# A third place for score products and products of zeros in TensorE's first waits, in a planned attention and mixture kernel

One Trainium2 chip, one core. The metric is the device time of one execution in microseconds (us), median of several runs; less is better.

## The reference

```python
# q, k, v: (8, 12, 448, 64)
scores = scale * np.matmul(q, k.transpose(0, 1, 3, 2))
m = np.max(scores, axis=-1, keepdims=True)
e = np.exp(scores - m)
attn = e / (np.sum(e, axis=-1, keepdims=True) + np.exp(-m) + 1e-09)
x = (attn @ v), heads side by side                # (3584, 768)
h = x @ w_in                                      # 768 -> 2048
P = a[0] + a[1] * h + a[2] * h**2 + a[3] * h**3
Q = 1.0 + np.abs(b[0]) * np.abs(h) + np.abs(b[1]) * h**2
out = (P / (Q + 1e-06)) @ w_out                   # 2048 -> 768
```

## The kernel before

The kernel writes its instructions in an order that a small planner in its own source finds while the kernel is built: every piece of work is an `Op` with an engine, an assumed duration and what it depends on, and `Plan.run` simulates the engines and takes the op that can start first. Twelve heads of a batch are three *quads* of four heads. For each quad TensorE makes eight score passes (K times Q, two heads side by side in two row tiles), ScalarE (ACT) takes exponentials of them, TensorE makes the sums (ones, then V in two halves), VectorE (DVE) multiplies by the reciprocal, and later come the dense products of x and w_in and of g and w_out. Score passes before batch 1 are cut in halves of 224 columns, so batch 0 has six half quads.

PSUM has eight banks: two score places of two banks each, `sps`, and four general banks, `gen`, for transposes, sums and dense products.

```python
sps = [ps.tile([128, 2, 512], F32, name=f"sps{i}") for i in range(NS)]      # NS = 2
gen = [ps.tile([128, 512], F32, name=f"gen{i}") for i in range(NGEN)]       # NGEN = 4
# ... in scores(), simplified:
    nc.tensor.matmul(
        out=sps[m % NS][0:128, hh, ci * qw:(ci + 1) * qw],
        lhsT=kt[n % NK][r, c0:c0 + 128],
        rhs=qt[n % NK][r, pr * S + q0:pr * S + q0 + qw], start=True, stop=True)
    nc.scalar.activation(out=e_sb[m % NE], in_=sps[m % NS][0:P, :, 0:S],
                         func=AF.Exp, scale=scale)
# ... from batch 3 on, passes are held back until two can go together:
    if b >= MB and t % 2:
        ops[t - 1].mate = s
```

The planner's knobs are tables of numbers: when each quad's attention is due (`DUE`, `DUES`), how far the products with w_out lag (`LAG`), and in which order weights and K, Q, V are loaded (`ORDER`; i is a piece of w_in, o of w_out, k is K and Q of a quad, v is V).

The softmax here doesn't subtract the row's maximum and nothing guards it: scores larger than these inputs give would overflow.

## Time and profile before

| | before |
|---|---|
| time, median of 4 runs | 431.44 us (430.86 to 431.57) |
| span of the profiled run | 429.0 us |
| TensorE / DVE / ACT busy | 418.3 / 339.7 / 327.9 us |
| products (matmul instructions) | 3680 |
| changes of kind on TensorE | 235 |
| time at full pace for all products | 386.8 us |

The last row is worked out: each product is given its columns at 2.4 GHz and 2.5 ns, as the Trainium skill has it ("TensorE: Matmul & The Clock Gate", "Wait — 56ns, not 53.3ns?"), halved for scores and transposes and quartered for sums, which run two and four side by side. That is 189 ns for 448 columns, where the trace shows 0.190. TensorE's records name their kind by source line, so a *change of kind* is a pair of neighbouring records of different kind among transposes, scores, sums and dense products (the first record is counted as one; where a kernel makes products of zeros, these count as a fifth kind).

From these two I read every trace as a ledger: the useful work that TensorE has done by a given moment, and the changes that it has paid for. What is left of a stretch after its useful work and 0.105 us per change was lost to waits or to a slow clock.

### The profile page before, as it was taken

The page shows a single profiled execution, that of the slowest core. Times are in us where ns is not written, and L with a number is a line of the kernel's source. Part 1 is how long each engine was busy: PE and PEld are TensorE (multiplying, and loading weights), DVE is VectorE, ACT ScalarE, POOL GpSimd, SP SyncE. Part 2 cuts the span into 40 slices and gives each one's busy share as a digit, 9 for nine tenths or more (in the row PEclk, how much of TensorE's full clock was granted, in tenths as well). Part 3 has the DMA queues.
Part 4 walks back from the last instruction along what each step waited for, and adds up shares of the span by engine and source line. Part 5 has one row for each costly group of instructions (what it writes and reads, how often), then busy time and mean ns, then how long its engine had stood idle before and what let it go on. Part 6 is the DMA issues. An engine that isn't in the chain of part 4 may idle for free.

```text
span 429.0 us, 8850 instructions
## 1 busy us (share of the span) xinstructions
PE 418.3 (98%) x3680; PEld 218.5 (51%) x3680; DVE 339.7 (79%) x513; ACT 327.9 (76%) x383; POOL 109.3 (25%) x170
## 2 busy tenths in 40 slices
PE   5899999999999999999999999999999999999996
PEld 2666664444444444455444455444444455555663
DVE  4437999999989997559987489984999999979500
ACT  4898999988999999744999984878878865585421
POOL 6555534543535203421206102320000100100000
PEclk9999999999999999999999999999999999999999
DMA  9999999999949833976339628914010101211222
GB/s 198 203 202 199 192 174 178 187 169 167 131 89 102 103 69 58 118 135 129 72 41 136 84 49 132 138 37 81 2 37 2 38 0 38 73 34 41 75 73 76
DMA packets 78185, 43.58 MB, mean 102 GB/s; under 512 B 36160, under 2 KB 74560, under 8 KB 78144
## 3 DMA queue, kind: packets, MB, share of 16 engines
q0 software_dynamic: 36928, 21.89, 38.9%
q1 hardware_dynamic: 39952, 20.26, 25.3%
q10 hardware_dynamic: 1264, 0.85, 0.7%
q8 instruction: 29, 0.48, 0.4%
q14 instruction: 12, 0.10, 0.1%
HBM read 45.62 MB, written 11.01 MB: 132 GB/s over the span
## 4 chain that ended last, share of the span: by engine, by line
PE 81%; DVE 14%; ACT 2%; DMA 1%; issue 1%; ACTq 0%; DVEq 0%
PE gen L716 33%; PE gen L618 29%; PE gen L552 11%; PE sps L517 8%; DVE h L635 3%; DVE n L655 2%; DVE n L659 2%; ACT e L525 2%; DVE c L659 1%; DMA g<-in_k_dram 1%; DVE g L659 1%; DVE x L580 1%; DVE c L655 1%; DVE w L655 1%; PE gen L433 0%
## 5 line engine op out<-in xcount | busy, mean ns | idle before, releaser
L525 ACT ACTIVATE e<-sps 112x896 f16<-112x896 f32 x192 | 167.5, 922 | 25.0 <-PE sps L517 24.2
L618 PE MATMUL gen<-x,w_in 128*128 128x448 f16 (+1 forms) x864 | 161.5, 332 | 0.0
L716 PE MATMUL gen<-w_out,g 128*128 128x384 f16 (+2 forms) x768 | 134.9, 326 | 0.0
L618 PEld LDWEIGHTS <-w_in 128*128 128x128 f16 x864 | 79.6, 98 | 70.8 <-issue 17.4
L716 PEld LDWEIGHTS <-g 128*128 128x128 f16 x768 | 73.3, 98 | 56.4 <-issue 7.5
L635 DVE CAST h<-gen 128x448 f16<-128x448 f32 x113 | 68.9, 617 | 19.0 <-PE gen L618 18.7
L659 DVE TENSOR_TENSOR n<-n,h 128x1792 f16<-128x1792 f16 x64 | 69.9, 1092 | 0.9
L670 ACT ACTIVATE c<-c,oneeps_c 128x1792 f16<-128x1792 f16 x32 | 57.4, 1794 | 16.2 <-DVE c L659 16.2
L738 ACT ACTIVATE o<-gen 128x384 f32<-128x384 f32 (+2 forms) x56 | 27.5, 492 | 44.6 <-PE gen L716 44.6
L517 PE MATMUL sps<-qt,kt 64*128 64x448 f16 (+1 forms) x432 | 57.9, 341 | 2.5 <-ACT e L525 1.2
L673 ACT ACTIVATE c<-c 128x1792 f16<-128x1792 f16 x32 | 54.7, 1709 | 0.3
L693 POOL COPY gx<-g 128x1024 f16<-128x1024 f16 x8 | 9.4, 1172 | 154.7 <-DVE g L659 154.7
L580 DVE TENSOR_TENSOR x<-gen,lden 128x448 f16<-128x448 f32 (+1 forms) x54 | 28.3, 563 | 21.1 <-ACT lden L568 17.1
L655 DVE TENSOR_SCALAR n<-n,abc 128x1792 f16<-128x1792 f16 x64 | 44.1, 689 | 1.0
L552 PE MATMUL gen<-e,vn 112*32 112x448 f16 (+1 forms) x864 | 41.8, 337 | 0.0
L659 DVE TENSOR_TENSOR g<-n,c 128x1792 f16<-128x1792 f16 x32 | 35.1, 1095 | 7.1 <-ACT c L673 6.2
L659 DVE TENSOR_TENSOR c<-c,w 128x1792 f16<-128x1792 f16 x32 | 35.0, 1094 | 0.1
L517 PEld LDWEIGHTS <-kt 64*128 64x128 f16 x432 | 14.7, 95 | 36.5 <-issue 33.1
L318 POOL DMA_DIRECT2D vn<-in_v_dram x24 | 18.1, 755 | 57.4 <-PE sps L517 43.9
L478 POOL COPY kp<-kn 112x256 uint32<-112x256 uint32 x36 | 19.5, 573 | 44.5 <-DMA kt<-kp 41.4
L552 PEld LDWEIGHTS <-vn 112*32 112x32 f16 x864 | 23.1, 99 | 14.0
L655 DVE TENSOR_SCALAR n<-h,abc 128x1792 f16<-128x1792 f16 x32 | 25.5, 797 | 0.3
(45 smaller groups left out, 249.2 us busy)
## 6 DMA issues: line engine op xcount, KB each, us to landing
vn<-in_v_dram POOLq DMA_DIRECT2D x24, 224.0 KB, 7.3
kn<-in_k_dram POOLq DMA_DIRECT2D x22, 224.0 KB, 7.8
qn<-in_q_dram POOLq DMA_DIRECT2D x22, 224.0 KB, 8.3
w_in<-in_moe_w_in_dram POOLq DMA_DIRECT2D x12, 256.0 KB, 10.2
w_out<-in_moe_w_out_dram POOLq DMA_DIRECT2D x4, 768.0 KB, 16.9
out_dram<-o SPq DMA_DIRECT2D x8, 336.0 KB, 3.2
out_dram<-o SPq DMA_DIRECT2D x8, 288.0 KB, 2.7
out_dram<-o SPq DMA_DIRECT2D x7, 240.0 KB, 2.5
```

The source lines that it names most:

```text
L517: nc.tensor.matmul(out=sps[m % NS][0:(P if i == 0 and j == 1 else 128), hh, ci * qw:(ci + 1) * qw], lhsT=kt[n % NK][r, c0:c0 + (P if i == ...
L525: nc.scalar.activation(out=e_sb[m % NE], in_=sps[m % NS][0:P, :, 0:S], func=AF.Exp, scale=scale)
L552: nc.tensor.matmul(out=gen[unit["bank"]][32 * h:32 * h + 32, 0:qw], lhsT=lhs(h, j), rhs=e_sb[m % NE][:, h % 2, c0:c0 + qw], start=(j == 0) ...
L580: mult.emit = lambda s=s, uu=uu: nc.vector.tensor_tensor(out=x_sb[b % NX][:, 2 * qd + s, q0:q0 + qw], in0=gen[uu["bank"]][:, 0:qw], in1=ld ...
L618: nc.tensor.matmul(out=gen[unit["bank"]][:, fi * qw:(fi + 1) * qw], lhsT=w_in_sb[wg][:, c // 2, c % 2, (fc % FG) * 128:(fc % FG + 1) * 128 ...
L635: nc.vector.tensor_copy(out=dst, in_=src)
L655: return lambda: nc.vector.tensor_scalar(out=out, in0=in0, scalar1=s1, scalar2=s2, op0=op0, **kw)
L659: return lambda: nc.vector.tensor_tensor(out=out, in0=in0, in1=in1, op=ALU.mult)
L670: lambda: nc.scalar.activation(out=c, in_=c, func=AF.Ln, bias=oneeps_c)))
L673: lambda: nc.scalar.activation(out=c, in_=c, func=AF.Exp, scale=-1.0)))
L716: nc.tensor.matmul(out=gen[unit["bank"]][:, 0:wd], lhsT=lhs, rhs=w_out_sb[f][:, fc % FG, cols], start=(fc == 0), stop=(fc == NFC - 1))
L738: nc.scalar.activation(out=o[:, cols], in_=gen[unit["bank"]][:, 0:wd], func=AF.Copy)
```

## The change

Three things are intended. A score pass that finds no free place may write two free general banks instead, one per head; then its exponential is cut in two, and the passes of a quad can be issued as 2, 3 and 3 instead of four times 2, from batch 2 on. While TensorE waits in the first 15.5 us, it makes products of a tile of zeros, so that its clock is released earlier. And all tables are found anew, with a planner that now counts TensorE at half pace up to 15.5 us.

```diff
+WAIT = 0.2 ... COLD = 15.5 ... WARM = 6.5 ... FILL = 0.048      # cut
+    def places(self, op):
+        out = [(h.end + 0.2 if h else 0.0, (i,)) for i, h in enumerate(self.slots)
+               if h is None or h.start is not None]
+        banks = self.bank_times()
+        if op.slot[2] and len(banks) >= GP:
+            out.append((banks[GP - 1][0] + 0.01, (banks[0][1], banks[1][1])))
+        return sorted(out)
...
+    def emit_fill(op, gap):
+        cols = op.dest()
+        for _ in range(int((gap - 0.08) / (FILL * (2 if op.start < WARM else 1)))):
+            nc.tensor.matmul(out=cols[0:64, 0:P], lhsT=idle[0:P, 0:64], rhs=idle[0:P, :],
+                             start=True, stop=True)
...
-    DUES = (0, 0, 4.2, 3.0)
+    DUES = (0, 0, 3.8, 3.8, 3.8, 0, 0, 0)
+    GROUPS = (2, 1, 3, 1, 1, 3, 1, 1)
+    START = ("ta tb s1 tc s0 s2 td s3 s5 s4 te A0 s7 s6 tf tg s9 s8 "
+             "A1 s10 s11 tl s12 s13 A2 s14 s15 s16 s17 A3 s18 s19 s20 s21 A4 s23 s22")
-    ORDER = "kikiikivkkvoovoovkvv"
+    ORDER = "kivkkvikiikovooovkvv"
...                                                # DUE and LAG: all values new
+                for hh in range(2):
+                    nc.scalar.activation(out=e_sb[m % NE][:, hh],
+                                         in_=gen[un["place"][hh]][0:P, 0:S],
+                                         func=AF.Exp, scale=scale)
...
     for op in plan.order:
+        if op.eng == "PE" and op.start < COLD:
+            if op.dest and op.start > end + 0.2:
+                emit_fill(op, op.start - end)
+            end = op.end if op.start < WARM else op.end - op.dur
         op.emit()
```

In `START`, s is a score pass, t a group of transposes, A the sums of a half quad. `op.dest` is the buffer that the op after the zeros will write.

More of the change, by code (lines that the diff above doesn't have):

```diff
@@ L24, in __init__ @@
         self.opens, self.kb, self.mode, self.lat = opens, kb, mode, lat
-        self.mate = None
+        self.slot = self.dest = None
+        self.group = 1
         self.start = self.end = self.land = None
@@ L31 @@
 SWITCH = 0.095
-WAIT = 0.5
+WAIT = 0.2
+GP = 2
+E_TWO = 0.2
+COLD = 15.5
+WARM = 6.5
+FILL = 0.048
 KB_US = 0.0027
@@ L49, in __init__ @@
         self.banks = [None] * banks
+        self.slots = [None, None]
         self.mode = None
@@ L99, in candidates @@
                 t = max(t, s[0])
+            if op.slot is not None:
+                places = self.places(op)
+                if not places:
+                    continue
+                s = places[0]
+                t = max(t, s[0])
             t = max(t, self.free[e])
@@ L104, in candidates @@
                 late = op.due > t
-                if name == "att" and op.mate is not None:
-                    tm = self.ready(op.mate)
-                    late |= tm is None or tm > t + WAIT
+                if op.group > 1:
+                    late |= len(places) < op.group or places[op.group - 1][0] > t + WAIT
                 if op.opens:
@@ L157, in run @@
             op.start = t
-            op.end = t + op.dur
+            op.end = t + op.dur * (2 if e == "PE" and t < COLD else 1)
             if e == "PE" and op.mode != self.mode:
@@ L165, in run @@
             self.pos[e, name] += 1
-            if s is not None:
+            if op.slot is not None:
+                unit, holder, _ = op.slot
+                unit["place"] = s[1]
+                if len(s[1]) == 1:
+                    self.slots[s[1][0]] = holder
+                else:
+                    holder.dur += E_TWO
+                    for i in s[1]:
+                        self.banks[i] = holder
+            elif s is not None:
                 _, unit, holder = op.gen
@@ L214 @@
     ones = const.tile([128, 32], F16, name="ones")
+    idle = const.tile([128, P], F16, name="idle")
     abc = const.tile([128, 6], F32, name="abc")
@@ L248, with place @@
     gen = [ps.tile([128, 512], F32, name=f"gen{i}") for i in range(NGEN)]
+    def place(unit, hh):
+        pl = unit["place"]
+        return gen[pl[hh]] if len(pl) > 1 else sps[pl[0]][:, hh]
     plan = Plan({
@@ L265, in emit_ident @@
         make_identity(nc, ident)
+    def emit_fill(op, gap):
[3 more added lines that the diff above has]
+                             start=True, stop=True)
     def emit_consts():
+        nc.vector.memset(idle, 0.0)
         nc.vector.memset(ones, 1.0)
@@ L289 @@
     PER = 1.95
-    DUES = (0, 0, 4.2, 3.0)
-    LEAD = 50.9
-    MB = 3
+    DUES = (0, 0, 3.8, 3.8, 3.8, 0, 0, 0)
+    GROUPS = (2, 1, 3, 1, 1, 3, 1, 1)
+    GB = 1
+    LEAD = 72.5
+    MB = 2
+    START = ("ta tb s1 tc s0 s2 td s3 s5 s4 te A0 s7 s6 tf tg s9 s8 "
+             "A1 s10 s11 tl s12 s13 A2 s14 s15 s16 s17 A3 s18 s19 s20 s21 A4 s23 s22")
     DUE = (
-        28.1, 39.7, 51.4, 58.5, 76.4, 91.4, 103.2, 87.5, 118.5,
-        129.9, 148.0, 129.5, 202.0, 155.9, 169.8, 134.0, 237.8, 280.8,
-        283.4, 262.8, 327.3,
+        29.7, 32.6, 39.6, 9.9, 62.9, 39.7, 101.8, 123.5, 140.9,
+        140.4, 169.9, 160.4, 189.3, 148.7, 221.8, 246.2, 253.0, 273.1,
+        291.1, 274.3, 297.0,
     )
     NPE = 6
-    TLEAD = 4.6
+    TLEAD = 0.1
     ACM = 100
@@ L445, in transpose_by_pe @@
                     src_op = first_casts[n, ti, pr, jh] if n < 2 else ld[n]
-                    tr = Op(f"t{n}", "PE", 0.4 / nh,
+                    tr = Op(f"t{n}", "PE", 0.21 / nh,
                             [src_op, ident_op, hist(qk_free, n, NK)], emit,
                             gen=(True, un, cp), mode="t")
+                    tr.dest = lambda un=un: gen[un["bank"]]
                     trs.append(tr)
@@ L510, in scores, with emit @@
                 chunks = [cc * jc + c for c in range(cc)]
-                def emit(pr=pr, chunks=chunks, m=m):
+                un = {}
+                def emit(pr=pr, chunks=chunks, un=un):
                     for ci, j in enumerate(chunks):
@@ L517, in emit @@
                             nc.tensor.matmul(
-                                out=sps[m % NS][0:(P if i == 0 and j == 1 else 128), hh,
-                                                ci * qw:(ci + 1) * qw],
+                                out=place(un, hh)[0:(P if i == 0 and j == 1 else 128),
+                                                  ci * qw:(ci + 1) * qw],
                                 lhsT=kt[n % NK][r, c0:c0 + (P if i == 0 and j == 1 else 128)],
@@ L522, in emit, with emit_e @@
                                 start=True, stop=True)
-                def emit_e(m=m):
-                    nc.scalar.activation(out=e_sb[m % NE], in_=sps[m % NS][0:P, :, 0:S],
-                                         func=AF.Exp, scale=scale)
+                def emit_e(m=m, un=un):
+                    if len(un["place"]) == 1:
+                        nc.scalar.activation(out=e_sb[m % NE],
+                                             in_=sps[un["place"][0]][0:P, :, 0:S],
+                                             func=AF.Exp, scale=scale)
+                        return
+                    for hh in range(2):
+                        nc.scalar.activation(out=e_sb[m % NE][:, hh],
+                                             in_=gen[un["place"][hh]][0:P, 0:S],
+                                             func=AF.Exp, scale=scale)
                 t = len(ops)
-                due = quad_due(n) + DUES[t // 2] * PER if b else 0.0
-                s = Op(f"s{m}", "PE", 0.19, ready_for(n, pr, jc, q0) + [hist(e_ops, m, NS)], emit,
+                due = quad_due(n) + DUES[t] * PER if b else 0.0
+                s = Op(f"s{m}", "PE", 0.19, ready_for(n, pr, jc, q0), emit,
                        due=due, mode="s", opens=t == 0 and i > 0)
                 ops.append(s)
-                if b >= MB and t % 2:
-                    ops[t - 1].mate = s
-                e_ops.append(plan.add("e", Op(f"e{m}", "ACT", 0.8,
-                                              [s, table, hist(e_free, m, NE)], emit_e,
-                                              due=due)))
+                if b >= MB:
+                    s.group = GROUPS[t]
+                e = plan.add("e", Op(f"e{m}", "ACT", 0.8, [s, table, hist(e_free, m, NE)],
+                                     emit_e, due=due))
+                s.dest = lambda un=un: place(un, 0)
+                s.slot = un, e, (t > 1 or i == 0) and b >= GB
+                e_ops.append(e)
         if q0 + qw == S:
@@ L564, in attend @@
                gen=(True, ud, ln), mode="a")
+        d.dest = lambda: gen[ud["bank"]]
         ln.deps = [d, hist(mults, i, 2)]
@@ L814 @@
     first = [op for op in trs[0] if not op.late]
-    late = [op for op in trs.pop(0) if op.late]
+    steps = {"ta": first[:2], "tb": first[2:3], "tc": first[3:], "td": trs[1][:2],
+             "te": trs[1][2:], "tf": trs[2][:2], "tg": trs[2][2:],
+             "tl": [op for op in trs[0] if op.late]}
+    halves_ = 2 * NQ
     prev = None
-    for i in range(len(units)):
+    for i, (b, qd, _, _) in enumerate(units):
         m0 = len(e_ops)
         passes = scores(i)
-        nu = units[i + 1] if i + 1 < len(units) else None
-        nxt = trs.pop(NQ * nu[0] + nu[1], []) if nu else []
-        if nu and nu[0]:
-            for op in nxt:
-                op.due = quad_due(NQ * nu[0] + nu[1]) - TLEAD
-                plan.add("tr", op)
-            nxt = []
-        more = {}
-        if i == 0:
-            more = {-1: first[:2], 0: first[2:3], 1: first[3:], 2: nxt[:2]}
-            rest = nxt[2:]
-        elif i < NQ:
-            more = {1: rest, 3: late if i == 2 else nxt}
-            rest = []
-        for op in more.get(-1, []):
-            plan.add("att", op)
-        for t, s in enumerate(passes):
-            plan.add("att", s)
-            for op in more.get(t, []):
-                plan.add("att", op)
-            if t == 1:
-                for op in prev or []:
-                    plan.add("att", op)
-        prev = attend(i, m0)
+        sums = attend(i, m0)
+        if i < halves_:
+            steps.update({f"s{m0 + t}": [s] for t, s in enumerate(passes)})
+            steps[f"A{i}"] = sums
+            if i == halves_ - 1:
+                for step in START.split():
+                    for op in steps[step]:
+                        plan.add("att", op)
+                prev = sums
+        else:
+            for op in passes[:2] + prev + passes[2:]:
+                plan.add("att", op)
+            prev = sums
+        n = units[i + 1][0] * NQ + units[i + 1][1] if i + 1 < len(units) else 0
+        if n >= NQ:
+            for op in trs.pop(n, []):
+                op.due = quad_due(n) - TLEAD
+                plan.add("tr", op)
     for op in prev:
@@ L855 @@
     LAG = (
-        (0, 3.5), (12.0, 1.8), (6.5, 2.4), (5.0, 1.9),
-        (4.0, 3.4), (12.0, 1.8), (11.5, 2.8), (12.0, 1.3),
+        (0, 3.8), (4.0, 2.2), (6.0, 4.0), (4.5, 2.3),
+        (10.5, 1.7), (6.0, 2.4), (12.0, 2.9), (18.5, 0.6),
     )
@@ L877 @@
     plan.run()
+    end = 1.0
     for op in plan.order:
+        if op.eng == "PE" and op.start < COLD:
+            if op.dest and op.start > end + 0.2:
+                emit_fill(op, op.start - end)
+            end = op.end if op.start < WARM else op.end - op.dur
         op.emit()
```

## The prediction

> **What bounds the kernel now.** I read the page first, then the table of engine time by stretch, then TensorE's timeline, then the chain.
>
> ```profile
> PE 418.3 (98%) x3680; PEld 218.5 (51%) x3680; DVE 339.7 (79%) x513; ACT 327.9 (76%) x383; POOL 109.3 (25%) x170
> ...
> PE 81%; DVE 14%; ACT 2%; DMA 1%; issue 1%; ACTq 0%; DVEq 0%
> ```
>
> TensorE is busy for 98% of the span and the chain that ended last runs on it for 81%, so the question is which of its time is lost. The table by stretch says where it idles:
>
> ```profile
> 0.00:15.00 15.00, 9.23 (x130) 5.61 (x132) 6.61 (x36) 7.71 (x10) 9.04 (x18) 1.00 1.08 199
> 15.00:30.00 15.00, 13.91 (x304) 9.68 (x302) 6.73 (x24) 14.33 (x21) 7.48 (x11) 1.00 1.32 204
> ...
> 60.00:75.00 15.00, 15.00 (x141) 8.18 (x139) 14.96 (x22) 14.61 (x17) 5.37 (x9) 1.00 1.35 174
> ...
> 150.00:200.00 50.00, 50.00 (x368) 25.41 (x367) 38.16 (x53) 36.50 (x42) 11.30 (x21) 1.00 0.60 99
> ```
>
> Columns: stretch, length, then busy us of PE, PEld, DVE, ACT, POOL. TensorE idles 5.8 us in the first 15, 1.1 in the next 15, then hardly until its last product (3.7 us of eviction and store end the kernel). Around 60 to 75 us DVE and ACT are as full as TensorE (the chain between 37 and 97 us does step through DVE); from 150 on they have a quarter to spare.
>
> A busy TensorE still loses time where it changes between kinds of product, as this piece of its timeline shows:
>
> ```profile
> 124.83 0.55 PE L517 MATMUL sps<-qt,kt 64*128 64x448 f16 x4
> 125.31 3.01 PE L618 MATMUL gen<-x,w_in 128*128 128x448 f16 x15
> 128.26 0.55 PE L517 MATMUL sps<-qt,kt 64*128 64x448 f16 x4
> 128.74 1.88 PE L618 MATMUL gen<-x,w_in 128*128 128x448 f16 x9
> 130.55 0.55 PE L517 MATMUL sps<-qt,kt 64*128 64x448 f16 x4
> ```
>
> From start to start 15 products of x and w_in take 2.95 us and 9 take 1.81, so one takes 0.190 and 0.10 is left over each time. Four score products take 0.48; two heads run side by side, so their own time is 2 x 0.190 = 0.38, and again 0.10 is left. Every change of kind therefore costs 0.10 to 0.11 us. Counting changes in the whole timeline gives about 235 (some 11 before 15 us, 22 to 30, 39 to 60, 38 to 105, 125 after), so about 25 us of the span. At my 0.190 per full row the products themselves need some 390 us.
>
> Last, the start, where the clock of the records is 1.00 and does not tell, but the pace does:
>
> ```profile
> 8.68 0.58 PE L433 MATMUL gen<-ident,kn 112*64 112x112 f16 x8
> 9.06 0.58 PE L433 MATMUL gen<-ident,qn 112*64 112x112 f16 x8
> ...
> 12.51 0.94 PE L552 MATMUL gen<-e,ones 112*32 112x224 f16 x16
> 13.24 1.71 PE L552 MATMUL gen<-e,vn 112*32 112x224 f16 x32
> 14.88 0.64 PE L517 MATMUL sps<-qt,kt 64*128 64x224 f16 x8
> ...
> 17.83 0.94 PE L552 MATMUL gen<-e,vn 112*32 112x224 f16 x32
> 18.71 0.37 PE L517 MATMUL sps<-qt,kt 64*128 64x224 f16 x4
> ```
>
> The same 32 products take 1.64 us at 13.24 and 0.88 at 17.83: TensorE runs at half pace up to about 14.9 us.
>
> **What the Trainium skill says.** "TensorE: Matmul & The Clock Gate", "What's actually happening": the array starts at half clock, and is released after a window of about 3.4 us of sustained work, the window running freely; Part 4 adds that transposes do not count as work in the same way. The trace agrees: TensorE is without a named wait only from 11.62, and 3.3 us later the pace doubles. "TensorEngine Tiling (Array Packing)", "Key Properties": changing the tiling mode drains the array; the trace has it at 0.10 to 0.11 us. The same page, "Gotcha 1: PSUM Pressure": different row tiles must write different banks, which is why a third place costs two whole general banks, one per head. "ScalarE: Activation LUTs", "What ACT_TABLE_LOAD costs": 186 ns + 0.833 ns per column, overlapping by 93 ns in sequence. That gives 0.93 us for 896 columns, the trace has a median of 0.917; an exponential cut in two should cost about 0.09 us more (an estimate from that page), where the kernel's planner is given 0.2.
>
> **The change part by part.**
>
> (1) Third place and groups. From batch 3 each quad now issues its eight score passes as 2+2+2+2; the change asks for 2+3+3 from batch 2. With the sums of the previous quad after the first group a quad costs the changes s, a, s, m, s, m, s, m = 8 (measured: 125 / 15 = 8.3), and then s, a, s, m, s, m = 6. Batches 3 to 7: 15 quads x 2.3 x 0.105 = 3.6 us, in stretches where DVE and ACT have slack, so all of it should come off the end. Batch 2 (38 changes for three quads, 12.7 each, passes mostly alone): up to 20 x 0.105 = 2.1 us, but there DVE and ACT are full, and TensorE time freed turns partly into waiting. I keep half, 1.0.
>
> (2) Its price. At most two cut exponentials per quad: some 40 x 0.09 = 3.6 us of ACT, or 8 at the planner's figure, over some 300 us with ACT at 75 to 85% mostly. Off the path except before 105 us. Two of four general banks are held for some 2 to 3 us (two exponentials ahead at 0.8 each, its own, the latency); meanwhile the dense products (1.13 us per 448-column unit) live on two banks and DVE must empty them behind 1.1 us elementwise rows. I charge 0.7 us for stalls.
>
> (3) Zeros in the waits. From about 1.1 us (memset first) TensorE runs products of zeros; first real work stays at 4.0, where the cast of K ends. A full window is over between 4.5 and 8 us; 6.5 is the middle and the constant of the change. In the old order the work between 6.5 and 14.9 us is 44 transposes, 20 score products and 48 sums. Warm savings: the sums 2.37 (12.51 to 14.88) against 1.27 (17.44 to 18.71), 1.1; transposes 8 in 0.38 against 0.20 (15.86 to 16.06), 1.0; scores 8 in about 0.95 against 0.57, 1.0. Together 3.1. Not all is on the path: ACT, which feeds the sums, waited 0.62, 0.53, 0.64, 0.81 and 0.99 us before its pieces from 7 to 15.4 us, 3.6 in all, but the first step also passes a landing of K at 8.2 us and DVE copies, and V of quad 0, issued at 4.52, lands near 11.8 (median 7.3 us). I take 2.2 us of earlier arrival at the seventh exponential, which then stays, because 15 to 25 us is a chain of exponentials at ACT's own pace.
>
> (4) The retuned order: scores of pass 1 before pass 0, sums later, w_in loads behind more K and V, due times of batches 1 and 2 earlier (quad 8 from 91 to 40 us), other lags. It removes no work. It moves ACT-heavy attention forward and dense work back, which should remove some of the 2 us that 60 to 105 us loses beyond its changes. I add 1.7 in all for it, the weakest term; it is set by a search in a model I do not run.
>
> Sum: 3.6 + 1.0 - 0.7 + 2.2 + 1.7 = 7.8 us, 431.36 - 7.8 = 423.6.
>
> **The rivals.** *The zeros delay the work.* A filler writes the buffer of the product it precedes. If that buffer is still being read, the filler waits too and then sits in front of real work; planned too long, it pushes the next transpose by up to a few tenths. For it: the count is from planned, not real, gaps. Against: gaps at the start are mostly waits for casts and DMA, with free buffers. This would eat 1 to 2 us: about 425.5. *Bank starvation.* Groups of three take two general banks when DVE is behind; TensorE then shows new waits for evictions. For it: DVE 99% at 60 to 75 us; against: the planner counts banks. If it bites everywhere, gains of (1) vanish: 427. *The start is bound by loads and ACT.* The DMA share is full up to 100 us and w_in now comes later; a warm array would wait for w_in or for exponentials: 426. *Everything lands.* Changes fall to some 170, 6.9 us, the start gives 3 us or more and the middle loses nothing: 419 to 420.
>
> **Range and chances.** The terms with a measured unit (groups, start) carry some 5 to 8 us, the rivals cost 1 to 4, the good case adds 3. So 423.6, with 418.5 to 428 for 8 in 10. Two per cent is 422.7, just under the middle: faster by over 2%: 0.41, within: 0.56, slower: 0.03 (a retune gone wrong on the chip).
>
> **What would show it.** Right: score runs of four and six products (2, 3, 3 passes) with gaps per change still 0.10 and about 180 changes; half-width exponentials of some 0.55 us next to 0.92; sums at 0.9 us per 32 by the first quad; dense start near 22.5 instead of 24.9 us. Wrong: half pace still at 10 us (zeros do not count), first transposes after 4.3 us (filler in the way), TensorE waits on evictions after 105 us (banks), or the first dense rows at 25 us or later (loads). If the middle, 37 to 105 us, gains more than 3 us, I undervalued the new order; the end is then under 421.

## The result

The changed kernel took 432.85 us (432.57 to 433.26, 4 runs), the kernel before 431.44. A ratio is always the mean time of one kernel's fast runs over that of the other's of the same rounds, so it is not quite the ratio of the medians; here it is 1.0036, 95% interval 1.0019 to 1.0053. The change is 0.4% slower, outside the predicted range of 418.5 to 428.

The page of the changed kernel, its busy times (PEld is TensorE's loading of weights) and its chain, which is the work that ended last, followed back step by step to what released it:

```profile
PE 420.0 (97%) x3781; PEld 227.1 (53%) x3781; DVE 340.8 (79%) x514; ACT 327.8 (76%) x423; POOL 108.0 (25%) x170
...
PE 80%; DMA 17%; DVE 2%; issue 0%; POOL 0%; ACT 0%
```

There are 101 products more (the zeros) and 40 exponentials cut in two at no cost in ACT's total. The chain now has 17% on DMA, where before it had 1%: it steps from the first loads over w_in to the last piece of w_out, which was issued at 44.2 and landed at 75.6 us. The same stretches as in the prediction (length, then busy us of PE, PEld, DVE, ACT, POOL, then clock, DMA share, GB/s):

```profile
0.00:15.00 15.00, 11.43 (x138) 9.25 (x139) 5.30 (x34) 5.24 (x6) 8.62 (x17) 1.00 1.08 196
15.00:30.00 15.00, 12.77 (x327) 9.46 (x331) 6.41 (x21) 12.90 (x21) 7.60 (x11) 1.00 1.38 202
...
60.00:75.00 15.00, 13.81 (x154) 8.82 (x147) 14.88 (x23) 15.00 (x18) 2.12 (x3) 1.00 1.32 177
...
150.00:200.00 50.00, 50.00 (x404) 24.53 (x402) 41.13 (x57) 39.65 (x53) 17.53 (x29) 1.00 0.67 106
```

TensorE is busier in the first 15 us (11.43 against 9.23), but with zeros, and ACT has done less (5.24 against 7.71). At 60 to 75 us TensorE now idles 1.2 us, most of it in one wait, from the list of TensorE's waits:

```profile
PE gen L778 <- DMA w_out<-in_moe_w_out_dram: 1.6, 1, 1.6
```

TensorE's timeline of the start, lines left out:

```profile
0.98 2.82 PE L308 MATMUL gen<-idle 112*64 112x112 f16 x28 [0.98 <-DVE idle L312]
...
8.21 0.56 PE L569 MATMUL sps<-qt,kt 64*128 64x224 f16 x4
9.77 2.86 PE L308 MATMUL sps<-idle 112*64 112x112 f16 x29 [1.01 <-ACT e L578]
12.57 0.49 PE L569 MATMUL sps<-qt,kt 64*128 64x224 f16 x4
...
15.07 0.80 PE L308 MATMUL sps<-idle 112*64 112x112 f16 x13
15.81 0.36 PE L569 MATMUL sps<-qt,kt 64*128 64x224 f16 x4
...
17.20 0.94 PE L613 MATMUL gen<-e,vn 112*32 112x224 f16 x32
```

And ACT's:

```profile
8.80 1.73 ACT L578 ACTIVATE e<-sps 112x896 f16<-112x896 f32 x2 [2.91 <-PE sps L569]
...
13.10 1.92 ACT L578 ACTIVATE e<-sps 112x896 f16<-112x896 f32 x2 [2.57 <-PE sps L569]
```

The third score pass is ready at 9.77, when the first exponential has emptied its place. The 29 zeros ahead of it write that same place, so they too wait for the exponential ("1.01 <-ACT e"), and only then take 2.8 us. The planner saw a gap of 1.49 us and at an assumed full pace put (1.49 - 0.08) / 0.048 = 29 there; the array was at half pace and they took twice that. ACT stands idle for 2.57 us meanwhile. At 15.07 the same happens again with 13 zeros, now at full pace. The first exponential starts at 8.80 us; before it started at 5.66:

```profile
5.66 0.90 ACT L525 ACTIVATE e<-sps 112x896 f16<-112x896 f32 x1
```

Full pace begins at 12.6 us instead of 14.9. The first dense product, on which DVE's dense work waits, comes 6.5 us later than before (first line before, second line changed):

```profile
24.86 0.75 PE L618 MATMUL gen<-x,w_in 128*128 128x224 f16 x6
31.31 1.32 PE L680 MATMUL gen<-x,w_in 128*128 128x224 f16 x12
```

Part of that is the planned order itself: in the changed kernel 192 products of sums stand ahead of the first dense product, where it was 144.

In the later part, the pattern of a quad:

```profile
220.30 0.55 PE L569 MATMUL sps<-qt,kt 64*128 64x448 f16 x4
...
221.54 1.69 PE L613 MATMUL gen<-e,vn 112*32 112x448 f16 x32
223.16 3.01 PE L680 MATMUL gen<-x,w_in 128*128 128x448 f16 x15
226.11 0.55 PE L569 MATMUL sps<-qt,kt 64*128 64x448 f16 x4
226.50 0.35 PE L569 MATMUL gen<-qt,kt 64*128 64x448 f16 x2
226.78 2.77 PE L778 MATMUL gen<-w_out,g 128*128 128x384 f16 x16
```

Groups of 2, 3 and 3 are there (the third pass writes `gen`), and the cost per change is as before (15 products in 2.95 us). But behind the sums now come dense products, not the next group: scores, sums, dense, scores, dense, scores, dense are seven changes per quad, not the six of the prediction.

The ledger of the two traces:

| by (us) | useful work before | after | difference | changes before | after |
|---|---|---|---|---|---|
| 15 | 3.77 | 1.94 | -1.83 | 11 | 17 |
| 30 | 14.26 | 10.53 | -3.73 | 33 | 41 |
| 60 | 39.30 | 36.63 | -2.67 | 72 | 74 |
| 75 | 52.54 | 48.87 | -3.67 | 90 | 84 |
| 105 | 80.02 | 76.80 | -3.22 | 110 | 98 |
| 394 | 355.75 | 353.16 | -2.59 | 235 | 211 |
| last product starts | 425.07 | 427.60 | 2.53 later | 235 | 211 |

In the changed kernel 19 of the changes up to 30 us are to or from zeros; without them its count is 22 at 30 us and 192 at the end. All of the loss is there at 30 us, and more. From 30 us to the end the changed kernel pays for 170 changes instead of 202, which is 32 x 0.105 = 3.4 us, and regains only 1.2; the stretch from 60 to 105 us loses 2.3 us beyond its changes, where before it lost 0.3.

### The profile page after: what moved, and what is told of

Its sections match the earlier page's. It is cut to its first block, busy times and chain, and to the rows that moved or that the text cites. A ratio compares the mean times of both kernels' runs of the same rounds, so it can differ in the third digit from the quotient of the medians.

```text
span 431.5 us, 9113 instructions
## 1 busy us (share of the span) xinstructions
PE 420.0 (97%) x3781; PEld 227.1 (53%) x3781; DVE 340.8 (79%) x514; ACT 327.8 (76%) x423; POOL 108.0 (25%) x170
## 4 chain that ended last, share of the span: by engine, by line
PE 80%; DMA 17%; DVE 2%; issue 0%; POOL 0%; ACT 0%
PE gen L778 33%; PE gen L680 30%; PE gen L613 9%; DMA w_out<-in_moe_w_out_dram 7%; DMA w_in<-in_moe_w_in_dram 7%; PE sps L569 6%; PE gen L569 2%; DMA kn<-in_k_dram 2%; DMA h<-in_k_dram 1%; DVE n L721 0%; DVE h L697 0%; DVE n L717 0%; DVE c L721 0%; DVE x L642 0%; DVE g L721 0%
## 5 line engine op out<-in xcount | busy, mean ns | idle before, releaser
L680 PE MATMUL gen<-x,w_in 128*128 128x448 f16 (+1 forms) x864 | 159.6, 332 | 0.3 <-DVE x L642 0.2
L578 ACT ACTIVATE e<-sps 112x896 f16<-112x896 f32 x152 | 133.6, 924 | 27.4 <-PE sps L569 27.0
L680 PEld LDWEIGHTS <-w_in 128*128 128x128 f16 x864 | 80.5, 98 | 69.0 <-issue 15.5
L569 PE MATMUL sps<-qt,kt 64*128 64x448 f16 (+2 forms) x352 | 45.3, 332 | 2.4 <-ACT e L578 1.9
L583 ACT ACTIVATE e<-gen 112x448 f16<-112x448 f32 x80 | 39.6, 560 | 0.0
L569 PEld LDWEIGHTS <-kt 64*128 64x128 f16 (+1 forms) x432 | 15.4, 95 | 31.1 <-issue 24.6
L717 DVE TENSOR_SCALAR n<-h,abc 128x1792 f16<-128x1792 f16 x32 | 26.4, 827 | 0.2
```

Source lines behind the costliest of these rows:

```text
L569: nc.tensor.matmul(out=place(un, hh)[0:(P if i == 0 and j == 1 else 128), ci * qw:(ci + 1) * qw], lhsT=kt[n % NK][r, c0:c0 + (P if i == 0 ...
L578: nc.scalar.activation(out=e_sb[m % NE], in_=sps[un["place"][0]][0:P, :, 0:S], func=AF.Exp, scale=scale)
L583: nc.scalar.activation(out=e_sb[m % NE][:, hh], in_=gen[un["place"][hh]][0:P, 0:S], func=AF.Exp, scale=scale)
L680: nc.tensor.matmul(out=gen[unit["bank"]][:, fi * qw:(fi + 1) * qw], lhsT=w_in_sb[wg][:, c // 2, c % 2, (fc % FG) * 128:(fc % FG + 1) * 128 ...
L717: return lambda: nc.vector.tensor_scalar(out=out, in0=in0, scalar1=s1, scalar2=s2, op0=op0, **kw)
```

## The experiments

The first theory, A, was that the zeros spoil the start because of the buffer they write. Its rivals were the order of the first scores, the loads, the third place. All runs had 5 rounds beside the kernel before, whose median was 431.1 to 431.4 each time. *Changed kernel* and *kernel before* name the two starting points.

### Changed kernel without zeros

```diff
-                emit_fill(op, op.start - end)
+                pass
```

> The changed kernel without one product of zeros; every other instruction and its order are the same. Theory A (a filler writes the buffer of the product that it precedes, so it waits for the same reader and then stands in front of the product: 29 of them at 9.77 to 12.57 us, 8 more at 6.1, 9 at 14.1, 13 at 15.1, 6 at 18.1): the first quads lose the 3 to 5 us that fillers cost, less what a later warm clock gives back; 430.0 us, 428.5 to 431.5, ratio to before 0.994 to 1.000; half pace until 14 us or later. Theory B (zeros pay for themselves and the start is slow through the order of its scores or through loads): no faster than the changed kernel, 432.8 or more, ratio 1.003 or more.

434.28 us, ratio 1.0080 (1.0058 to 1.0102): slower than with zeros. Yet the ledger says what A said of the start: at 30 us it is 2.01 us behind the kernel before instead of 3.73, so the zeros do cost 1.7 us there. The gain is gone at 75 us, where the ledger reads 48.87, the very value of the changed kernel: the last piece of w_out lands at 75.4 us here and at 75.6 there, and TensorE just waits 2.9 us for it. Behind that wait the kernel is worse:

```profile
75.46 1.44 PE L778 MATMUL gen<-w_out,g 128*128 128x384 f16 x4 [2.93 <-DMA w_out<-in_moe_w_out_dram]
...
76.00:80.00 4.00, 4.00 (x17) 1.90 (x16) 1.18 (x2) 3.06 (x5) 2.73 (x6) 0.71 1.48 198
```

The granted clock (the share of full speed that the throttle let through) is 0.71 between 76 and 80 us, and all six runs have a mean of 0.994 to 0.996, where the changed kernel's four have 0.998 to 1.000. So A was right about the start and wrong about the time.

### Changed kernel with zeros in free banks

```diff
+                op.spare = [i for i, h in enumerate(self.banks) if h is None or
+                            h.start is not None and h.end + 0.5 <= self.free[e]]
...
-        cols = op.dest()
+        if not op.spare:
+            return
+        cols = gen[op.spare[-1]]
```

> The changed kernel with the same number of zeros at most, written to a general bank that the plan holds free, never to the buffer of the next product. Theory A: the zeros now run inside the waits; full pace from 7 to 9 us instead of 12.6, seventh exponential 3 us earlier; 429.0 us, 427.5 to 430.5, ratio 0.991 to 0.998, and not slower than without zeros. Theory B: destination does not matter, 432.8. Theory C (zeros do not count as work for the clock): half pace as without zeros, and a time within 0.1% of that kernel.

434.45 us, ratio 1.0071 (1.0046 to 1.0096). The zeros now run inside the wait:

```profile
8.78 1.98 PE L313 MATMUL gen<-idle 112*64 112x112 f16 x29
10.69 0.36 PE L574 MATMUL sps<-qt,kt 64*128 64x224 f16 x4
```

The third pass starts 1.9 us earlier than in the changed kernel, and at full pace. At 30 us the ledger is 2.10 behind instead of 3.73; at 75 us it is 3.51 behind, TensorE having waited 2.6 us for w_out, and the clock is 0.77 from 76 to 80 us. Same story. Here the single runs fall in two: the four with a mean clock of 0.996 took 434.39 to 436.26 us, the two at 1.000 took 433.26 and 432.09, about level with the changed kernel. So the median hides some 2 us between executions with and without a cold array. What the clock alone costs is not shown by that, since a shorter wait would spare both; a run further down isolates it.

### Changed kernel with the loads in the old order

```diff
-    ORDER = "kivkkvikiikovooovkvv"
+    ORDER = "kikiikivkkvoovoovkvv"
```

> The changed kernel with the loads of w_in, w_out, K, Q and V in the order of before. Theory L (the late w_out, on which TensorE waits 1.6 us at 74 us, and the late w_in cost the middle): that wait goes, 431.0 us, ratio to before 0.997 to 1.001, ledger between 30 and 105 us better by 1 to 2 us. Rival (the order of loads is even, the plan uses TensorE otherwise meanwhile): 432.3 to 433.3.

435.31 us, ratio 1.0092 (1.0073 to 1.0110). This edit leaves the order of TensorE's products as it was, record for record. The wait for w_out is gone, as expected, and still the time is no better. TensorE's waits from 60 to 110 us are now for DVE, in small pieces:

```profile
PE gen L778 <- DVE h L697: 0.5, 2, 0.3
PE gen L569 <- DVE x L642: 0.5, 1, 0.5
PE gen L680 <- DVE x L642: 0.5, 2, 0.3
```

DVE (third busy time) has nothing left from 60 to 105 us:

```profile
60.00:75.00 15.00, 14.68 (x160) 9.32 (x153) 14.93 (x22) 15.00 (x18) 4.66 (x8) 1.00 1.35 175
75.00:90.00 15.00, 14.55 (x118) 6.58 (x117) 15.00 (x21) 13.89 (x18) 8.91 (x11) 1.00 1.49 156
90.00:105.00 15.00, 14.71 (x120) 7.07 (x118) 14.93 (x20) 12.13 (x16) 6.16 (x11) 1.00 1.05 130
```

With the late start (3.83 us behind at 30) DVE gets its first dense unit late (32.7 us, as in the changed kernel; before it was 28.4), and it has little to spare until 150 us. At 105 us the ledger reads 76.80 again. I had taken the wait for the cause; it was the one that came last of two. Why it is 2.5 us slower than the changed kernel (1.2 in the traces, all of it after 105 us, where 1.5 us are lost to 150 instead of 0.5), the runs do not settle. The first dense product is at 31.4 us here and 31.3 in the changed kernel, so w_in's later loads do not hold it back.

### Changed kernel without the third place

```diff
-    GB = 1
+    GB = 99
-    GROUPS = (2, 1, 3, 1, 1, 3, 1, 1)
+    GROUPS = (2, 1, 2, 1, 2, 1, 2, 1)
```

> The changed kernel without a third place, score passes in groups of two from batch 2; zeros, loads, lags and due times as changed. If groups of three are worth what the count of changes of kind says (12 fewer after 105 us, 20 fewer from 30 to 105, at 0.105 us): 1.3 to 3.4 us slower than the changed kernel, 434.2 to 436.3. If the third place costs more in held banks and cut exponentials than it saves: 432.8 or less.

438.98 us, ratio 1.0181 (1.0164 to 1.0198). 252 changes instead of 211 explain 4.3 of the 6.1 us that it is slower than the changed kernel; the other tables were found for groups of three. So within its own plan the third place is worth a good deal, but this does not isolate it.

### Both repairs together

New theory, M: the start sets when DVE gets work; loads and DVE bound the middle in turn; a repair of one alone is swallowed by the other. This run has zeros in free banks and the old order of loads.

> The changed kernel with both undone at once: zeros in free banks (start 2 us earlier in the trace, but the time not better, because TensorE then waited 2.8 us for w_out at 72 us) and loads in the order of before (the w_out wait gone, but the time not better, because the start was still late and DVE full from 45 to 150 us). Theory M (the start sets when DVE gets its first dense unit; loads and DVE bound the middle in turn, so each repair alone is swallowed): together they come through, 2 us under the kernel with the loads alone: 432.0 to 433.5, ratio 1.002 to 1.005. Rival N (the loss lies after 105 us, in lags and due times tuned for another order): 434.5 or more.

431.98 us, ratio 1.0016 (1.0001 to 1.0031), at the lower edge of the range that M gave. Neither edit alone gained anything (434.45 and 435.31), and together they are clearly faster than either. Against the changed kernel they gain 0.9 us, with intervals that overlap. The ledger at the end is 1.46 behind instead of 2.59. TensorE's order is the same in all four kernels, so that the two edits depend on each other is shown. That it is DVE which carries the late start on is argued, from its busy time and its first dense unit (31.4 us here); no run made DVE's work lighter.

### The same, with batch 0 in the old order

```diff
+START = "ta s0 tb s1 tc s2 td s3 s4 s5 te A0 s6 s7 tf tg s8 s9 A1 ..."     # as before
```

> As the last, and with the score passes, transposes and sums of batch 0 in the order of before (pass 0 first, so the first exponential at about 5.8 instead of 8.8 us, first dense product at 24 us or earlier). Theory M: a further 1 to 2.5 us, 430.0 to 432.0, ratio 0.997 to 1.001. Rival N: no better than the last one, within 0.5 us.

435.55 us, ratio 1.0105 (1.0083 to 1.0126): a miss. The start is mended, 0.85 us behind at 30 us, but from 30 to 60 us 3.44 us are lost beyond the changes, 2.9 of them in two waits of score passes for exponentials at 47 and 57 us:

```profile
PE sps L574 <- ACT e L583: 2.9, 2, 2.0
```

The edit does more than its name says: from the new start the planner chose another order later on as well, and only 1,873 of TensorE's 3,680 products stand at the same place as in the run before. The due times of batches 1 and 2 suit another start; that this is the reason is argued, not shown.

### Kernel before with the third place alone

```diff
-GROUPS = (2, 1, 2, 1, 2, 1, 2, 1), GB = 99
+GROUPS = (2, 1, 3, 1, 1, 3, 1, 1), GB = 1
```

> The kernel before with the third place and groups of 2, 3, 3 from batch 3, and nothing else (no zeros, due times, lags, loads, start as before). If the third place is worth 1 to 2 changes of kind per quad at 0.105 us: 1.3 to 3.2 us faster, 428.2 to 430.1, ratio 0.993 to 0.997; changes after 105 us 95 to 112 instead of 125. Rival (held banks and cut exponentials cost as much, or the old due times do not suit it): 431 or slower.

435.28 us, ratio 1.0096 (1.0077 to 1.0114): a miss again, with 216 changes instead of 235. Up to 200 us it is level with the kernel before; then it stalls:

```profile
222.24 2.32 PE L680 MATMUL gen<-x,w_in 128*128 128x448 f16 x9 [1.97 <-DVE x L642]
```

Just before, at 217.9 to 219.5, the sums had filled two general banks and at 219.9 a third pass the other two. All four were held. The multiplication that frees the first two waited for the reciprocal, which ACT did behind a logarithm of 1.8 us for the dense part (219.25 to 221.06), and the exponentials that free the other two came after it. Dense products had no bank until 222.2. That is the rival of starvation, in one instance. The wait of 1.97 us also cooled the array:

```profile
224.00:228.00 4.00, 4.00 (x17) 1.35 (x16) 1.13 (x3) 4.00 (x6) 0.00 (x0) 0.64 0.00 0
```

Read in steps of 1 us, the clock is 0.50 to 0.54 from 224 to 227 us. So part of the 3.1 us lost between 200 and 250 us is cold array and not held banks. My trial was also unfair: its due times, one per pair, cut groups of three apart, and the planner itself puts its last product at 428.8 us, where it puts that of the kernel before at 424.6.

### Kernel before with zeros alone, in free banks

This is the changed source with all tables of before. Without the zeros, TensorE's 3680 products stand in the trace in the order of before, but for two records that are exchanged; this run adds 67 zeros to that.

> The kernel before with zeros alone: 67 products in its planned waits, in free banks, order of everything else unchanged to the instruction. If a warm array at the start is worth what I predicted: full pace at 8 to 10 us instead of 14.9, seventh exponential 1.5 to 2.5 us earlier, 429.0 to 430.0, ratio 0.994 to 0.997. Rival (the start is bound by landings and by ACT, or what it gains is swallowed by loads and DVE before 105 us): 431.0 to 431.9, ratio 0.999 to 1.001.

430.91 us, ratio 0.9997 (0.9977 to 1.0016). The ledger is 0.53 us ahead at 30 us and 0.94 at 55, then 0.10 behind at 65:

```profile
PE sps L574 <- DMA qt<-qp: 0.9, 1, 0.9
```

In this trace a transposed Q that lands at 64 us took all of it.

### Kernel before with the same zeros, in the buffer of the next product

> The kernel before with the same 67 zeros as in the run with zeros in free banks, but written as the change writes them, to the buffer of the next product. Theory A2 (the buffer makes the filler wait with the product and then delay it; 39 of the 67 stand ahead of score passes or sums): the start loses 1 us or more against free banks, useful work at 30 us 0.5 to 1.5 us behind instead of 0.5 ahead; since delays, unlike gains, are not swallowed by the landing at 63 us if they are larger than it, 431.5 to 433. Rival (destination does not matter here): 430.9, ledger as with free banks.

430.53 us, ratio 0.9982 (0.9969 to 0.9995): slightly faster than the kernel before, against my expectation. Here the planned waits are short (at most 9 zeros each), and the ledger at 30 us is 0.48 ahead, as with free banks. So the buffer alone is not what hurts. As these runs read, it hurts where many zeros stand before a product that waits for that buffer. Here no late landing shows in the trace, and the 0.5 us stay to the end. Full pace comes between these two records, some 5 us sooner than without zeros:

```profile
8.75 0.56 PE L569 MATMUL sps<-qt,kt 64*128 64x224 f16 x4
...
10.40 0.37 PE L569 MATMUL sps<-qt,kt 64*128 64x224 f16 x4
```

### Changed kernel without zeros, pass 0 first

```diff
-    START = ("ta tb s1 tc s0 s2 td ...
+    START = ("ta s0 tb s1 tc s2 td ...
```

> The changed kernel without zeros and with score pass 0 before pass 1 (the first seven steps of the start only); compare with the changed kernel without zeros (434.3). If the late first exponential (8.6 us, behind a cast of K that ACT does behind its table load) is what makes its start slow: first exponential at 5.8 us, ledger at 15 us level with before instead of 0.6 behind, at 30 us 1.0 instead of 2.0 behind. The time will not show it (w_out at 75 us takes it): 433.5 to 435. Rival: the ledger at 30 us is unchanged, because the first dense product waits for sums or w_in.

433.84 us, ratio 1.0052 (1.0028 to 1.0077), and the ledger as expected: level at 15 us, 0.95 behind at 30 instead of 2.01. With pass 1 first, the first exponential has to wait for a cast of K that ACT does behind its table load; that order costs 1.1 us. In this trace the gain over the run without zeros is still there at 75 us (1.0) and at 394 (1.4), w_out having landed at 73.8 us and not at 75.4; so that landing is not the same in every execution or order. In time the gain is 0.4 us by the medians and 1.2 by the ratios, with intervals that overlap. Again the runs fall in two: four with a mean clock of 0.995 or 0.996 took 433.53 to 435.19, two at 1.000 took 431.21 and 432.91.

### New tables for the kernel before, with and without the third place

For both I let the kernel's own planner search for tables from the values of before, equally long. It promised last products at 427.3 (third place) and 427.5 us (pairs).

> Start, loads and zeros of before (none), third place with groups of 2, 3, 3 from batch 3, and due times, lags and lead found anew for it, by the kernel's own planner, from the values of before. Its planned changes of kind are 214 (before 234). If the third place is worth its changes once the plan suits it: 428.5 to 430.5 and faster than its twin without a third place by 0.5 to 1.5 us. Rival (bank starvation cannot be planned away): no faster than the twin, stalls of TensorE on multiplications and casts of DVE after 105 us.

> The twin: same start, loads, same search of the same length, groups of two and no third place. Planned changes 225. A retune alone: 429.5 to 431.5. If it is faster than the kernel with the third place, the third place has no worth of its own here.

439.38 us (ratio 1.0184) and 434.19 us (1.0064). Both start badly: at 30 us the ledgers are 4.49 and 1.52 us behind, the first with waits of transposes for K and Q that the planner did not see, and behind them a cold array (granted clock 0.50 from 28 to 32 us). In the traces the last products start at 434.0 and 429.3 us. The comparison is worthless for the third place; what it shows is that the planner is wrong by 2 to 7 us after a search, more than anything under study here. The two starting points agree with that: for the kernel before, the planner of its own source puts the end of the last product at 424.6 us, and the trace has its start at 425.1; for the changed kernel it says 424.0, and the trace has 427.6. In that plan the third score pass stands at 8.57 us (12.57 in the trace) and the last piece of w_out lands at 68.0 (75.6).

### Zeros in the wait for w_out

```diff
+                if (b, tl, nh, f) == (0, 0, 0, NG - 1):
+                    for _ in range(52):
+                        nc.tensor.matmul(out=gen[unit["bank"]][0:P, 0:P], lhsT=idle,
+                                         rhs=idle, start=False, stop=False)
```

This is the changed kernel without zeros at the start. The new products add zero to an accumulation that is under way.

> The changed kernel without zeros at the start, and with 52 products of zeros (2.5 us at full pace) that add nothing to the accumulation which waits for the last piece of w_out at about 72 us. If the 2.9 us wait let the array go cold (granted clock 0.71 from 76 to 80 us, products 0.16 us longer each), the clock stays at 1.00 there and 1.0 to 1.5 us come back: 432.8 to 433.4, ratio 1.003 to 1.006. Rival (the loss behind the wait is bank or DVE bound): 434.0 to 434.6.

432.99 us, ratio 1.0039 (1.0026 to 1.0051), 1.3 us better than without them, as expected. The clock at 76 to 80 us is whole:

```profile
75.17 0.81 PE L782 MATMUL gen<-w_out,g 128*128 128x384 f16 x4
...
76.00:80.00 4.00, 4.00 (x24) 1.79 (x23) 2.84 (x4) 3.98 (x6) 2.36 (x7) 1.00 1.44 195
```

Four products that took 1.23 us behind the wait (75.46 to 76.69) now take 0.65 (to 75.82). So an earlier arrival at a landing that had not moved (75.4 us against 75.6) did not merely gain nothing: the longer wait cooled the array and cost 1.3 us. It also shows that zeros count as work for the clock.

### Kernel before with zeros and a third place with due times per group

```diff
+    DUES = (0, 0, 2.5, 2.5, 2.5, 5.0, 5.0, 5.0)      # on the run that gave 430.53;
+                                                    # GROUPS and GB as in the change
```

> The kernel before with the 67 zeros (as in the run that gave 430.5), plus the third place and groups of 2, 3, 3 from batch 3 with due times 0, 4.9 and 9.8 us after the quad's. If groups of three pay (213 planned changes against 234): 428.5 to 430.0, ratio 0.993 to 0.997. Rival (starvation: sums hold two general banks, the third place two more, dense units wait for a multiplication that waits for ACT): 431.5 or slower, stalls of 1 to 2 us on DVE x after 105 us.

432.87 us, ratio 1.0045 (1.0032 to 1.0058), 2.3 us slower than without. Against that run it has 21 changes fewer (227 against 248), 2.2 us, but between 30 and 394 us it loses 5.6 us beyond its changes instead of 1.4, in pieces of up to 0.7 us, several of them behind DVE.

### Both repairs and pass 0 first

```diff
-    START = ("ta tb s1 tc s0 s2 td ...
+    START = ("ta s0 tb s1 tc s2 td ...          # on the run that gave 431.98
```

> The changed kernel with zeros in free banks, loads in the old order and pass 0 before pass 1. If the start carries through once loads no longer stop it: 1.0 us under the run without the last edit (432.0): 430.5 to 431.5, ratio 0.998 to 1.001. Rival (DVE takes it between 60 and 105 us): 432.0 or more.

430.08 us, ratio 0.9976 (0.9957 to 0.9995): the lowest median, though its interval does not set it apart from the kernel before with zeros (0.9969 to 0.9995). Here the new start changed little else: 3,644 of TensorE's 3,680 products stand where they stood. DVE's first dense unit comes at 29.6 us. The ledger is 1.05 us behind at 30, level at 55 us and 1.3 ahead at 394. After 30 us it pays for 166 changes instead of 202 (3.8 us saved) and loses 1.4 us more beyond them than the kernel before. So the third place and the tables found for it, which no run separates, are together worth some 2.4 us after 30 us, once the loads do not stop them; a start that is 1.05 us late takes part of it back.

## Why the prediction was wrong

The prediction summed 3.6 + 1.0 - 0.7 + 2.2 + 1.7 = 7.8 us; measured was a loss of 1.4 (2.5 in the traces). By its steps:

- **Step (3), the zeros, failed in sign.** Predicted was 2.2 us of earlier arrival; the start came 3.7 us later by the ledger. The zeros themselves cost 1.7 (changed kernel against the two runs without them or in free banks), the new order of the first passes 1.1 (pass 0 first), and about 0.9 is left over that no run takes apart. The loads and the order of batch 0 are not in it: with both as before and the zeros in free banks, the ledger is still 0.85 behind at 30 us. The later place of the first dense product in the plan, which that run shares (192 sums ahead of it instead of 144), is a candidate that was not tested. The rival *the zeros delay the work* was described rightly, down to the buffer, and priced at 1 to 2 us; I argued it away with free buffers, where the long wait was one for an exponential. The rival *the start is bound by loads* did not come true for w_in, though its sign did: the first dense product came at 31.3 us instead of the 22.5 foretold, but at 31.4 with the old loads too, at 28.1 without the zeros and with pass 0 first. The mechanism behind the 2.2 us was real, but later than the 4.5 to 8 us foretold: the clock is released by zeros at about 10 us in the kernel before and at 12.6 in the changed one (half pace at 10 us was my sign for zeros that do not count; they do). And it is worth 0.5 us at 30 us, not 2.2, even with the old order. That term was four times too large.
- **Step (1), the count of changes, was mis-sized.** The cost of a change, 0.105 us, held. I expected 55 fewer after 30 us and counted 32: 20 of the 20 up to 105 us came, but only 12 of the 35 after it. There a quad has seven (113 for 15 quads, 7.5 each) and not six, since behind the sums comes dense work. As I read the plan, that is so because the sums hold two general banks and a third pass would take the other two; the prediction gave these two banks a stall of 0.7 us and no change of order. (It also put the two banks down to the row tiles alone; by the kernel's own shapes, two heads of 448 columns do not fit in one bank of 512.) The trial with the third place alone showed what happens otherwise, a stall of 2 us.
- **Step (2), the price.** The cut exponential was nearly free, as estimated (two halves in 0.98 us against one of 0.92). The banks were the price, as I read it, but hidden in the plan as changes not saved.
- **Step (4), the new order, failed in sign.** I gave it 1.7 us for the middle. The stretch from 60 to 105 us lost 2.3 us beyond its changes instead of 0.3, 1.6 of it in the wait for w_out. That wait was the last of two limits: with the old loads it is gone and the stretch still loses 2.3, and 2.2 with both repairs; with pass 0 first as well it loses 1.1. I had read in the diff that weights load later, put it down as a rival, and added a gain all the same.
- **The sum itself failed.** I added an early start to later gains as though the middle would pass them on. It does not always: w_out at 75 us and, in one trace, a transposed Q at 64 us took early gains away, and so, as far as its waits show, did DVE, 95% busy or more from 45 to 150 us. Of the three repairs to the start and the loads, the two run alone with the changed kernel gave nothing in time, two together gave 0.9 us, three 2.8. And a gain that ended in a wait of 2.9 us cost 1.3 us of cold array.
- **Right** were the reading that TensorE's lost time is changes and start, the groups in the trace, and the warning that the retune is the weakest term. My test for banks (waits on evictions after 105 us) was not met in the changed kernel, since its tables avoid them.

What stays open: the last 0.9 us of the start, why the old order of loads alone is 2.5 us slower than the changed kernel, what the third place is worth apart from its tables, whether DVE alone carries a late start on, and whether a search on the chip and not in the planner would make more of the third place.

## What to carry to other kernels

A filler must not depend on what the waiting instruction waits for; where it shares that instruction's buffer, it runs after the wait and not in it. Before an early gain is added to a sum, look for the next landing or full engine downstream and ask what would be left there, and how long the wait will be: here waits of 2.0 to 2.9 us cost the clock as well, in some or all executions. Read the mean clock of each single run, too: it parted the runs of two kernels here by some 2 us that the median hides. Tables found by a planner carry its errors, so a retune is to be priced by the planner's record on the chip (here off by 2 to 7 us), not by its promise.

## What the Trainium skill lacked or had wrong

- "TensorE: Matmul & The Clock Gate" gives an idle window of about 3.4 us (and a rule of about 3 us) before the array goes cold. A wait of 2.9 us was enough: granted clock 0.71 in the 4 us after it, four products in 1.23 us instead of 0.65. So was one of 1.97 us (0.64 in the 4 us from 224 us on, kernel before with the third place alone); one of 2.04 us was not (1.00, with batch 0 in the old order), nor one of 1.6 us (the stretch from 75 to 90 us of the changed kernel is at 1.00). In two kernels whose traces have a wait of 2.6 and 2.7 us there, the mean clock was lower in four of six runs each.
- The same page does not say whether products of zeros release or hold the clock. They do: full pace from about 10 us instead of 14.9 with 67 zeros, and 1.00 instead of 0.71 with 52 zeros in the wait.
- The granted clock in the records did not show the cold start at all (1.00 from 0 to 15 us, at half pace), but did show the cooling at 76 us. No page names this case; pace has to be read from the distance of records.
- "TensorEngine Tiling (Array Packing)" says that a change of tiling mode drains the array, without a figure. Here a change between kinds of product cost 0.10 to 0.11 us where it was read off; at 0.105 for each of the 202 changes from 30 to 394 us, only 1.3 us of that stretch are left unexplained.
- "ScalarE: Activation LUTs" leads to 0.09 us for cutting an exponential of 896 columns in two; two halves took 0.98 us against 0.92 for the whole, so the cut cost 0.06.
